# Loading a weight matrix by columns instead of by rows, with a new order of all steps, in a one-core attention and MLP kernel

## The chip, the core and the metric

The kernel runs on one core of one Trainium2 chip. Its time is the device time of one execution in microseconds. The core has five engines that work side by side: PE (TensorE, the matmuls; its weight loads are shown as PEld), DVE (VectorE), ACT (ScalarE), POOL (GpSimd) and SP (SyncE, which here only starts DMA transfers). Each engine goes through its own list of instructions in order. An instruction that needs something from another engine or from a transfer waits on a semaphore, and all that stands behind it on that engine waits with it.

## The reference

Attention in two scales on q, k, v of 8 batches, 8 heads, 576 positions and 64 features, and then an MLP on the 4608 tokens:

```
q_d, k_d, v_d = means of q, k, v over 4 positions        # 144 of 576
out  = repeat(softmax(q_d k_d' / 8) v_d, 4)              # coarse
out += softmax(q k' / 8 where |i - j| < 4) v             # local
x = out as 4608 tokens x 512
h = x @ w_in                                             # 512 x 2048
g = where(h > 0, h, exp(min(h, 0)) - 1)
y = g @ w_out                                            # 2048 x 512
```

All inputs and outputs are float32 in the chip's main memory; the matmuls run on float16.

## The kernel before

**Tiling.** A batch has four pairs of heads (j = 0 to 3), which are transposed, scored and normalised pair by pair. The results go into `xt`, the MLP's input with features on partitions, 512 tokens to a block t; a pair's 128 features are one of four row blocks dc of `w_in`. The first layer of block 0 is made in steps `h.0.i` and the other blocks' in `h.t.i`; the ELU takes `he` and `hg`, and the second layer `y` or, from block 6 on, a form with seven products (`p`, `sm`, `wd`).

**The order.** A string `ORDER` holds 1531 keys, each a step on some engines (`lc.1.0.q`: POOL starts the casting load of batch 1, pair 0, q; `T`: transposes; `fN`, `fna`: normalise batch 0 on DVE and add it into `xt` on POOL; `cv`: POOL's cast of a v). The keys are run from first to last, and this sets the order of the instructions on each engine. A stroke behind a key picks another way to do the step: another engine for an elementwise operation, or transposes by DMA instead of on PE. `SLOTS` tells which buffer each tile takes.

**The first weights.** `WI` holds `w_in` as one float16 tile of 128 partitions x 4 row blocks dc x 2048 columns. The keys `wi.0` to `wi.3` run `load_wi(dc)` (L345): one casting transfer each on POOL's queue, for one row block with all 2048 columns. The order issues them as wi.1, wi.2, wi.0, wi.3. `w_in(dc, fc)` takes 128 columns, four apart, out of the group of 512 columns that `fc // 4` names.

**The partial products ahead.** While batch 0 is still being normalised pair by pair, PE runs the keys `H.0` to `H.3` (`ahead(dc)`, matmuls at L891): for h.0.0 and h.0.1, that is fc 0 to 3, the partial product with row block dc alone. Each is four matmuls of 128 x 256. They read columns 0 to 511 of row block dc. Behind them stand `fO` (the outputs of a pair half), and the transposes `T.1.n` of batch 1.

**Fills.** `Z.0` to `Z.3` (`more_zeros`) are two matmuls of zeros each, 128 x 512, between the first steps on PE; `zeros` begins with thirteen such, and others of the kind (`lg<-Z`) stand in front of some `fO`.

**Semaphores of POOL's loads.** The casting loads that POOL starts take eight semaphores, DMASW0 to DMASW7, in turn. A wait for one of them is a wait for a certain load on it.

Of the kernel before, what the change touches and what calls it, by code (L numbers as in the profile page):

```python
# [41 lines left out]
lc.0.2.q zeros Z.3 lv.0.1 lc.0.2.k empties cIND cN cI cR T.0.2.(0,2) ek.0.2' edges sq.2.q eq.0.2 sk.2.k'  # L42
s.2.1.2 lc.0.1.k lc.0.1.q T.0.1.(0,0) s.2.0.2 lv.0.3 lx.0.0.k lx.0.0.q lx.2.3.q lv.0.0 close eq.0.1' ek.0.1
sk.1.k cx.0.0.k sq.1.q' s.1.0.0 cx.0.0.q T.0.0.(1,0) sq.0.q' ek.0.0' x.2.0 x.1.0 eq.0.0 s.1.1.0 x.1.1 sk.0.k
s.0.0.1 x.0.0 cv.0.3 lc.0.3.q lc.0.3.k wi.1 Z.2 T.0.3.(0,0) sq.3.q' Z.1 eq.0.3' ek.0.3' fD.0.0 Z.0 cVR2 cVR
lv.0.2 cIND2 sk.3.k' s.3.0.1 x.3.0 cv.0.0 cSEL lc.1.0.q wi.2 lc.1.2.q wi.0 wi.3 lc.1.3.q cv.0.1 cv.0.2 fdr.0
# [5 lines left out]
T.1.3 ek.1.3' cv.1.1' eq.1.3 T.1.2 h.0.15 h.0.10 eq.1.2 he.0.8 he.0.15 hg.0.5' sk.1.1 lx.2.0.k sk.1.3 hg.0.15
sq.1.2' lx.2.0.q sq.1.1 sq.1.3 s.1.3 sd.1.3 ek.1.2 he.0.10 x.1.3.0 sk.1.2 hg.0.8 wo.2 sq.1.0 cv.1.2 cv.1.3
lv.2.0 wo.1 cx.2.0.q lx.2.2.q' cx.2.0.k cv.2.0 h.0.3 s.1.1 sd.1.1 x.1.1.0 x.1.1.1 x.1.3.1 h.0.9 he.0.9'
hg.0.10 hg.0.9' s.1.2 sd.1.2 x.1.2.0 m.1.2 m.1.3 m.1.1 fna.2.1' lv.2.2 s.1.0 sd.1.0 h.0.2 x.1.2.1 x.1.0.0
he.0.2 x.1.0.1 he.0.3' m.1.0 hg.0.2 lx.2.2.k hg.0.3' V.1 h.0.11 h.0.12 D.1 vc.1 he.0.11' he.0.12 y.0.0 dr.1
P.1.1 P.1.3 pc.1.3' h.0.4 pc.1.1 P.1.2 on.1.1 of.1.1 hg.0.12 pc.1.2 T.2.0 y.0.1 eq.2.0 ek.2.0 hg.0.11' n.1.1
P.1.0 h.0.14 on.1.3 of.1.3 he.0.4' pc.1.0 he.0.14' y.0.4 y.0.5 on.1.0 of.1.0 a.1.1.1' a.1.1.2' sk.2.0 n.1.3
a.1.3.1' hg.0.4' lv.2.1 lv.3.1 wo.3 cx.2.1.q cx.2.1.k a.1.3.2 fna.3.1 cv.2.1' cx.2.2.q' cx.2.2.k n.1.0 on.1.2
of.1.2 hg.0.14' n.1.2 a.1.2.1' a.1.0.1 lx.2.3.k y.0.6 T.2.1 y.0.7 T.2.2' h.1.0 y.0.2 h.1.1 ek.2.1' yc.0.1'  # L60
eq.2.2 ek.2.2 eq.2.1 he.1.0 s.2.0 lx.3.2.q lx.3.1.k lv.2.3 sq.2.0' sd.2.0 he.1.1' sk.2.2 hg.1.0 sq.2.2'
hg.1.1' sk.2.1 x.2.0.0 s.2.2 y.0.3 h.0.13 lx.3.1.q lx.3.0.k ys.0.1 x.2.0.1 cv.2.2 cx.2.3.q cx.2.3.k cv.2.3'
cx.3.0.k lx.3.0.q lv.3.0 lv.3.2 lx.3.2.k h.1.5 he.1.5 yc.0.0 sq.2.1' hg.1.5 h.1.3 he.1.3' he.0.13 fl.3.0
lx.3.3.k T.2.3 sd.2.2 ek.2.3 a.1.2.2 cx.3.0.q cv.3.0 cx.3.1.k cx.3.1.q a.1.0.2 x.2.2.0 x.2.2.1 y.0.12 hg.0.13
y.0.13 h.1.7 hg.1.3' m.2.0 sk.2.3 m.2.2 he.1.7 cv.3.1' cx.3.2.k cx.3.2.q hg.1.7 y.0.8 s.2.1 sd.2.1 y.0.14
ys.0.0 eq.2.3 x.2.1.0 x.2.1.1 h.1.4 T.3.0 he.1.4' h.1.2 y.0.9 he.1.2' m.2.1 sq.2.3' eq.3.0' hg.1.4' lv.4.0
fl.3.1 lx.3.3.q lv.3.3 lx.4.0.q' lx.4.0.k s.2.3 sd.2.3 T.3.1 sq.3.0 cv.3.2 cx.3.3.k cx.3.3.q fl.3.2 fl.3.3
x.2.3.0 x.2.3.1 hg.1.2' eq.3.1' sq.3.1 m.2.3 h.1.6 y.0.15 T.3.2 D.2 V.2 he.1.6 eq.3.2 hg.1.6 dr.2 h.1.8 vc.2
yc.0.3 P.2.2 P.2.1 h.1.11 pc.2.1' pc.2.2 he.1.8' sk.3.1 hg.1.8' on.2.1 of.2.1 y.1.0 P.2.0 h.1.9 y.0.10
he.1.11' he.1.9' n.2.1 pc.2.0' hg.1.11' on.2.0 of.2.0 s.3.1 sd.3.1 n.2.0 hg.1.9' a.2.0.3' h.1.13 P.2.3 cv.3.3  # L70
a.2.1.3 a.2.0.2 x.3.1.0 x.3.1.1 sk.3.0 lx.4.3.q'' a.2.1.2 pc.2.3 he.1.13' h.1.12 on.2.2 of.2.2 sq.3.2 n.2.2
# [1379 lines left out]
```

## Time and profile before

| What | Value |
|---|---|
| median of 3 runs | 340.17 us (339.78 to 340.57) |
| profiled execution | 339.14 us, span 337.3 us, mean granted PE clock 0.994 |
| PE busy | 326.0 us, 97% of the span |
| DVE busy | 253.1 us, 75% |
| ACT busy | 210.2 us, 62% |
| POOL busy | 165.4 us, 49% |
| moved by DMA | 49.06 MB, 145 GB/s over the span |

The profile comes from one execution. Its own time, 339.14 us, is 1.03 us below the median of the three timed runs, and 1.8 us of it lie outside the span. Busy times of the engines overlap; what counts is which engine has no gap in a stretch, and what ended its gaps where it has some. A row of the windows view gives, for a stretch from A to B, its length and the busy time (with the number of instructions) of PE, PEld, DVE, ACT and POOL, then the granted PE clock, the share of DMA that was busy and the GB/s moved. A row of the timeline gives start, duration, engine, line, operation, out<-in, and in brackets how long the engine stood idle before it and what released it. The profile's line numbers are those of the kernel before; the changed one's are 3 lower there (L888 is L891), and 6 to 8 lower near the end.

### The profile page before, as it was taken

To read this page: it belongs to the slowest core of one execution; us is meant where nothing else is said; L and a number is where in the kernel's file an instruction comes from. 1 tells how busy PE (TensorE), PEld (TensorE's weight loads), DVE (VectorE), ACT (ScalarE), POOL (GpSimd) and SP (SyncE) were. 2 spreads that over 40 slices of the span, in tenths; PEclk is the share of its full clock that TensorE was granted. 3 is DMA by queue.
4 is the path that set the end of the run, shared out by engine and by line. 5 is a ranking of instruction groups with operands and counts; after the bars stand their busy time and mean duration, and the time that the engine had idled before them with its cause. 6 is when DMAs were issued, how large, how long until landed. Compare 5 with 4: busy or idle time off the path is not lost.

```text
span 337.3 us, 10747 instructions
## 1 busy us (share of the span) xinstructions
PE 326.0 (97%) x4418; PEld 194.3 (58%) x4418; DVE 253.1 (75%) x495; ACT 210.2 (62%) x369; POOL 165.4 (49%) x261
## 2 busy tenths in 40 slices
...
GB/s 166 232 207 205 193 202 207 199 220 168 188 190 203 136 235 187 157 216 195 165 175 201 175 201 173 109 168 76 31 67 92 65 31 2 0 127 0 1 126 124
DMA packets 109746, 49.06 MB, mean 145 GB/s; under 512 B 93937, under 2 KB 104193, under 8 KB 109697
## 3 DMA queue, kind: packets, MB, share of 16 engines
...
q0 software_dynamic: 5312, 7.15, 12.8%
q8 instruction: 34, 0.56, 0.7%
q10 hardware_dynamic: 240, 0.11, 0.2%
q14 instruction: 15, 0.12, 0.1%
...
## 4 chain that ended last, share of the span: by engine, by line
PE 72%; DVE 8%; DMA 7%; POOL 5%; issue 4%; SPq 2%; ACT 1%; DVEq 0%; POOLq 0%; ACTq 0%
PE hp L915 30%; PE op L956 20%; PE y L1028 6%; PE xz L1028 5%; DMA q<-in_q_dram 5%; DMA v<-in_v_dram 2%; PE lg L795 2%; DVE gt L946 2%; PE den L703 1%; PE sc L643 1%; SPq L452 1%; DVE xt L879 1%; POOL v L477 1%; PE hp L891 1%; DVE e L945 1%
## 5 line engine op out<-in xcount | busy, mean ns | idle before, releaser
L915 PE MATMUL hp<-xt,WI 128*128 128x512 f16 x512 | 127.7, 381 | 0.4 <-DVE gt L946 0.3
L956 PE MATMUL op<-WO,gt 128*128 128x512 f16 x384 | 95.1, 379 | 0.4 <-DVE gt L946 0.4
L915 PEld LDWEIGHTS <-WI 128*128 128x128 f16 x512 | 55.3, 114 | 44.4 <-issue 1.1
L941 DVE SCALAR_TENSOR_TENSOR gt<-e,hp 128x512 f16<-128x512 f16 x76 | 51.6, 682 | 23.6 <-ACT e L937 23.5
L936 ACT ACTIVATE r<-hp 128x512 f32<-128x512 f32 x76 | 45.4, 597 | 35.3 <-PE hp L915 34.1
L926 ACT ACTIVATE e<-hp 128x512 f16<-128x512 f32 x68 | 40.3, 597 | 32.0 <-PE hp L915 30.4
L956 PEld LDWEIGHTS <-gt 128*128 128x128 f16 x384 | 36.0, 98 | 41.6 <-DVE gt L946 1.1
L937 ACT ACTIVATE e<-r 128x512 f16<-128x512 f32 x76 | 47.9, 631 | 2.4
L946 DVE SCALAR_TENSOR_TENSOR gt<-hp,e 128x512 f16<-128x512 f32 x68 | 47.0, 692 | 2.7
L879 POOL TENSOR_TENSOR xt<-ln 128x128 f16<-128x128 f16 (+7 forms) x35 | 24.0, 695 | 42.6 <-DVE ln L868 42.6
L945 DVE TENSOR_SCALAR e<-e 128x512 f16<-128x512 f16 x68 | 24.2, 356 | 20.9 <-ACT e L926 20.6
L666 ACT ACTIVATE pex<-sc 128x580 f16<-128x580 f32 (+1 forms) x56 | 31.2, 596 | 6.8 <-PE sc L656 6.7
L1006 POOL TENSOR_TENSOR s<-gt 128x512 f16<-128x512 f16 x8 | 9.4, 1176 | 34.4 <-DVE gt L941 12.3
L415 POOL CAST k<-k 96x768 f16<-96x768 f32 x22 | 18.3, 831 | 15.8 <-DMA k<-in_k_dram 15.8
L477 POOL CAST v<-v 128x640 f16<-128x640 f32 (+1 forms) x19 | 14.1, 744 | 23.2 <-DMA v<-in_v_dram 23.0
L415 POOL CAST q<-q 96x768 f16<-96x768 f32 x20 | 16.6, 832 | 12.6 <-DMA q<-in_q_dram 8.7
L1028 PEld LDWEIGHTS <-gt 128*128 128x128 f16 x192 | 18.8, 98 | 4.8
L868 DVE TENSOR_TENSOR ln<-lg,rcb 128x580 f16<-128x580 f32 x28 | 21.0, 751 | 0.0
L561 DVE TENSOR_REDUCE ke<-kt 128x145 f16<-128x580 f16 x28 | 20.8, 750 | 0.0
L891 PE MATMUL hp<-xt,WI 128*128 128x256 f16 x128 | 16.3, 274 | 1.5 <-DVE gt L946 0.9
L579 POOL TENSOR_TENSOR t<-qt 128x288 f32<-128x288 f16 x16 | 10.6, 665 | 13.0 <-DVE qt L543 8.1
L1028 PEld LDWEIGHTS <-s 128*128 128x128 f16 x144 | 14.1, 98 | 3.4
...
## 6 DMA issues: line engine op xcount, KB each, us to landing
v<-in_v_dram SPq DMA_DIRECT2D x111, 80.0 KB, 4.8
...
WI<-in_moe_w_in_dram POOLq DMA_DIRECT2D x4, 512.0 KB, 8.9
WO<-in_moe_w_out_dram POOLq DMA_DIRECT2D x4, 512.0 KB, 6.4
```

Source lines behind the costliest of these rows:

```text
L415: nc.gpsimd.tensor_copy(out=x[:], in_=src)
L666: nc.scalar.activation(out=s["p"][:, :, a : a + n], in_=g2(sc, a, n), func=AF.Exp, scale=SCALE / 16 if a else SCALE,)
L879: (eng or nc.gpsimd).tensor_tensor(out=xt(t)[:, j, t0 - TBLK * t : t1 - TBLK * t], in0=ln[:, a:z], in1=_rep4(ln[:, ga : ga + (z - a) // 4] ...
L915: nc.tensor.matmul(hp, w_in(dc, fc), xts[t][:, dc, :], start=(dc == 0), stop=(dc == DMC - 1),)
L926: nc.scalar.activation(out=e, in_=hp, func=AF.Exp)
L936: nc.scalar.activation(out=r, in_=hp, func=AF.Relu, scale=-1.0)
L937: nc.scalar.activation(out=e, in_=r, func=AF.Exp, scale=-1.0)
L941: nc.vector.scalar_tensor_tensor(out=to, in0=e, scalar=-1.0, op0=AB.add, in1=hp, op1=AB.max)
L945: nc.vector.tensor_scalar(out=e, in0=e, scalar1=1.0, scalar2=-1.0, op0=AB.min, op1=AB.add)
L946: nc.vector.scalar_tensor_tensor(out=to, in0=hp, scalar=0.0, op0=AB.max, in1=e, op1=AB.add)
L956: nc.tensor.matmul(op_[:], gts[t][:, fc, 128 * tt : 128 * tt + 128], WO[:, fc, :], start=(fc == 0), stop=(fc == FCN - 1),)
L1028: nc.tensor.matmul(to, w, x, start=(k == 0 and n in (1, 2)), stop=(k == FH - 1), skip_group_check=n > 2,)
```

## The change

`load_wi(n)` now loads a group of 512 columns over all four row blocks, in place of a row block over all columns. The fills `Z` are gone. The order of all steps is another one, 278 steps have another form, and the buffers follow. Four keys go (the fills), so 1527 are left. The order now issues wi.0 first, then wi.2 and wi.3, and wi.1 last.

```
     def load_wi(dc):
-        nc.gpsimd.dma_start(out=WI[:, dc, :], in_=moe_w_in[128 * dc : 128 * dc + 128])
+        n = slice(512 * dc, 512 * dc + 512)
+        nc.gpsimd.dma_start(out=WI[:, :, n], in_=moe_w_in[:, n].rearrange("(c p) f -> p c f", p=128))
...
-    def more_zeros(n):
-        keep(two("zf"), 2)
-
...
-    for n in range(4):
-        at("Z", more_zeros, n)
...
 ORDER = """
-fD.2.0 fN.1 fdr.2 H.0 H.1 fna.1.0 lc.1.1.k fD.3.0 fP.2.0 fO.2.0 fpc.2 fdr.3 fN.2 fna.2.0 lc.1.2.k H.2 H.3
-fP.3.0 h.0.0 h.0.7 fO.3.2 h.0.1 he.0.0 fpc.3' hg.0.0 fN.3 he.0.7 he.0.1' T.1.0 h.0.5 cv.1.0 fna.3.0 wo.0
+s.3.1.0 fD.1.0 fD.2.0 fN.0 fna.0.0 x.3.1 lv.1.3 fdr.1 fdr.2 fP.1.1 fD.3.0 fV.2 H.0 fP.2.0 fpc.2 lx.2.1.q fdr.3
+fvc.2' fpc.1' fO.1.4 fN.1 fO.3.2 fP.3.0 fpc.3 fN.3 fna.1.0 cv.1.0 wi.1 H.1 H.2 H.3 fO.2.0 T.1.1 h.0.0 h.0.1
```

**On PE, at the partial products.** WI is the weight, xt the moving operand, hp the partial product; DMASW names the semaphore of the load that is waited for. Before, H.0 waits for wi.0 (DMASW2), H.1 for wi.1 (DMASW6), H.2 for wi.2 (DMASW0) and H.3 for wi.3 (DMASW3):

```order
L748 MATMUL den<-pex,IND 32x72
L891 LDWEIGHTS WI [waits DMASW2_49]
L891 MATMUL hp<-xt,WI 128x256 [waits Pool_49]
...
L891 LDWEIGHTS WI [waits DMASW6_49]
...
L834 MATMUL lg<-pex,vd 64x72
L891 LDWEIGHTS WI [waits DMASW0_49]
L891 MATMUL hp<-xt,WI 128x256 [waits Pool_49]
...
L891 LDWEIGHTS WI [waits DMASW3_49]
```

Now H.0 waits for wi.0 alone (DMASW6), and the first weights of H.1 wait for three semaphores:

```order
L888 LDWEIGHTS WI [waits DMASW6_49]
L888 MATMUL hp<-xt,WI 128x256 [waits Pool_49]
...
L760 MATMUL rb<-rch,SEL 128x72
L888 LDWEIGHTS WI [waits DMASW7_49,DMASW6_49,DMASW1_49]
L888 MATMUL hp<-xt,WI 128x256
...
L824 MATMUL lg<-pex,v_459 64x96 [waits DVE_49]
...
L505 LDWEIGHTS q_475 [waits DMASW2_49]
```

What moved: H.0 stands by itself earlier, and H.1, H.2 and H.3 stand together behind fP.3.0 (the rb matmuls), ahead of fO.2.0 (lg) and the first transposes of batch 1 (tqk). The wait of H.1 names the semaphores that wi.3 (DMASW7), wi.2 (DMASW6) and wi.1 (DMASW1) use; no first-layer weight behind it waits for a load of WI.

**On POOL, at the loads of WI.** xt<-ln is fna, CAST v is cv, the 1x1 COPY belongs to cv. Before, all four pieces are issued ahead of the first fna; the three that follow wi.1 stand like this:

```order
L374 DMA q_534<-in_q_dram 96x2x384 [waits DMASW0_49,PE_49]
L345 DMA WI<-in_moe_w_in_dram 128x2048
L374 DMA q_537<-in_q_dram 96x2x384 [waits DMASW3_49,DMASW1_49,PE_49]
L345 DMA WI<-in_moe_w_in_dram 128x2048 [waits DMASW2_49]
L345 DMA WI<-in_moe_w_in_dram 128x2048
L374 DMA q_541<-in_q_dram 96x2x384 [waits DVE_49,DMASW4_49,PE_49,Activation_49]
```

Now wi.2, wi.3 and wi.1 stand like this:

```order
L342 DMA WI<-in_moe_w_in_dram 128x4x512 [waits DMASW6_49]
L342 DMA WI<-in_moe_w_in_dram 128x4x512 [waits DMASW7_49]
L371 DMA q_490<-in_q_dram 96x2x384 [waits DMASW0_49]
L851 ISA
L851 TENSOR_TENSOR xt<-ln 128x2x288 [waits DVE_49] x2
L474 CAST v_847<-v_503 128x640 [waits DMAHW6_49,DMAHW7_49,DMAHW1_49,DMAHW0_49]
L401 COPY apart<-v_847 1x1 [waits Pool_49]
L342 DMA WI<-in_moe_w_in_dram 128x4x512 [waits DMASW1_49]
```

What moved: the last piece, wi.1, went behind both fna.0.0 and fna.1.0, which wait for DVE's fN.0 and fN.1, and behind the cast cv.1.0.

More of the change, by code (lines that the diff above doesn't have):

```diff
@@ L41 @@
 ORDER = """
[L42 to L46, printed above, removed]
@@ L52 @@
[L52 to L56, printed above, removed]
@@ L57 @@
[L57 to L71, printed above, removed]
@@ L147 @@
-sm.8.2.3' pk.8.0.7' sm.8.3.3' pf.8.1.4 pk.8.0.1 p.8.0.6.0 p.8.0.4.0 p.8.1.5.0 p.8.0.6.1 pk.8.0.6' p.8.1.5.1
-pf.8.1.5 p.8.0.4.1 p.8.0.5.0 p.8.0.5.1 ps.8.1.5 pf.8.0.4 pf.8.0.5 ps.8.0.5 p.8.1.3.0 p.8.1.3.1 pf.8.1.3
-ps.8.1.3 p.8.0.3.0 p.8.0.3.1 pf.8.0.3 ps.8.0.3
+lc.0.2.q cI lc.0.2.k cR zeros T.0.2.(0,2) lx.0.0.q eq.0.2 empties ek.0.2' edges sq.2.q cN cVR2 lx.0.0.k cVR
+cIND2 lv.0.0 sk.2.k' lc.0.1.q lc.0.1.k s.2.0.2 T.0.1.(0,0) lc.0.3.k lc.0.3.q s.2.1.2 close eq.0.1' sk.1.k'
+cx.0.0.k ek.0.1' sq.1.q x.2.0 cx.0.0.q T.0.0.(1,0) sq.0.q' eq.0.0' s.1.0.0 ek.0.0 x.1.0 s.1.1.0 sk.0.k
@@ new lines @@
+he.0.1 he.0.0' lv.1.2 fN.2 ek.1.1' fna.3.0' eq.1.1' sq.1.1 lx.2.3.q' fna.2.0 fna.2.1 T.1.0 h.0.5 he.0.5'
+hg.0.1 hg.0.0' lx.2.0.q cMASK lx.3.1.q sk.1.1 fna.3.1' ek.1.0 sk.1.0 hg.0.5' h.0.7 T.1.3 eq.1.3 eq.1.0 h.0.6
+T.1.2 ek.1.2' wo.1 wo.0 sq.1.3 cv.1.1 ek.1.3 he.0.6' h.0.8 h.0.15 he.0.8 eq.1.2 he.0.15 sq.1.2 sq.1.0 lv.2.0
+sk.1.3 hg.0.6' lx.2.0.k s.1.1 sd.1.1 s.1.3 cv.1.2 cv.1.3 hg.0.8 lx.2.2.k hg.0.15 sk.1.2 lv.2.1 lx.2.1.k cFOUR
+cx.2.0.q sd.1.3 h.0.10 h.0.12 x.1.3.0 x.1.1.0 x.1.3.1 x.1.1.1 he.0.7 wo.2 cx.2.0.k cv.2.0 hg.0.7 s.1.0 s.1.2
@@ new lines @@
+sd.1.0 he.0.12 he.0.10 x.1.0.0 hg.0.10 lx.2.2.q' h.0.9 he.0.9' h.0.3 sd.1.2 hg.0.9' x.1.0.1 x.1.2.0 he.0.3'
+m.1.0 m.1.3 m.1.1 hg.0.3' hg.0.12 V.1 h.0.2 h.0.11 y.0.0 x.1.2.1 m.1.2 D.1 he.0.11' hg.0.11' dr.1 he.0.2'
+vc.1' hg.0.2' h.0.4 P.1.3 P.1.1 pc.1.3' h.0.14 he.0.4' pc.1.1 on.1.1 of.1.1 n.1.1 y.0.1 P.1.0 pc.1.0 T.2.0
+on.1.3 of.1.3 hg.0.4' a.1.1.1' n.1.3 ek.2.0 eq.2.0 sq.2.0' sk.2.0 a.1.1.2' a.1.3.2' y.0.4 P.1.2 wo.3 cx.2.1.q
+cx.2.1.k cv.2.1' cx.2.2.q' cx.2.2.k a.1.3.1 pc.1.2 he.0.14' lv.3.1 lx.2.3.k lv.2.2 lx.3.1.k on.1.2 y.0.5
@@ new lines @@
+on.2.0 of.2.0 h.1.9 he.1.9 yc.0.3 s.3.1 sd.3.1 h.1.13 y.1.0 n.2.0 hg.1.9 sk.3.2 a.2.0.3' a.2.1.3 a.2.0.2
+a.2.1.2 lx.4.2.k' fl.3.3 lv.4.1 lx.4.1.k' lx.4.1.q on.2.2 of.2.2 x.3.1.0 he.1.13' x.3.1.1 n.2.2 h.1.12 he.1.12
+hg.1.13' hg.1.12 P.2.3 pc.2.3 y.0.11 s.3.0 sd.3.0 on.2.3 of.2.3 m.3.1 n.2.3 x.3.0.0 x.3.0.1 cv.3.3 cx.4.0.k
+cx.4.0.q a.2.2.2 h.1.14 he.1.14 y.1.1 T.3.3 h.1.10 eq.3.3 hg.1.14 sk.3.3 he.1.10' hg.1.10' sq.3.3 a.2.3.3
+s.3.2 h.1.15 s.3.3 sd.3.3 sd.3.2 a.2.3.2 he.1.15' x.3.3.0 x.3.2.0 y.1.2 h.2.0 hg.1.15' m.3.0 x.3.2.1 x.3.3.1
@@ new lines @@
+h.2.8 he.2.8' cv.4.0' yc.0.2' y.1.3 T.4.0' ys.0.3 eq.4.0'' lx.4.2.q fl.4.0 lv.4.2 m.3.3 m.3.2 yc.1.0' cx.4.1.k
+cx.4.1.q cv.4.1 cx.4.2.k cx.4.2.q T.4.1'' V.3 vc.3' he.2.0' hg.2.0' hg.2.8' D.3 sq.4.0' dr.3 fl.4.1' y.1.4
+y.1.5 h.2.4 y.1.6 eq.4.1 s.4.1 h.2.5 he.2.4' sq.4.1 lx.4.3.k lx.5.3.q' y.1.7 sk.4.1 hg.2.4' he.2.5 h.2.1
+cv.4.2' yc.1.1 he.2.1 cx.4.3.k hg.2.5 sk.4.0 y.1.8 so.3 ys.0.2 lv.4.3 si.3 s.4.0 sd.4.1 sd.4.0 h.2.2 y.1.12
+cx.4.3.q' x.4.1.0 hg.2.1 he.2.2 x.4.1.1 hg.2.2 x.4.0.0 cv.4.3' x.4.0.1 h.2.7 T.4.2'' h.2.10 m.4.0 on.3.0
@@ new lines @@
+he.3.1 hg.3.1 cx.5.3.k a.3.3.4 cx.5.3.q a.3.1.4 h.3.15 y.2.10 he.3.15 so.4 T.5.3' ys.1.2 eq.5.3'' lx.6.0.q'
+si.4 fl.5.3 lv.6.1 ys.2.1 on.4.0 of.4.0 of.4.3 y.2.13 h.3.7 he.3.7' hg.3.15 n.4.3 sq.5.3' hg.3.7' h.3.5
+he.3.5' s.5.0 sd.5.0 n.4.0 hg.3.5' y.2.11 h.3.11 y.2.14 h.3.8 on.4.2 he.3.11 x.5.0.0 x.5.0.1 on.4.1 of.4.1
+of.4.2 yc.2.2' he.3.8' hg.3.11 a.4.0.5' a.4.3.5 sq.5.2 cv.5.3' cx.6.0.k' cx.6.0.q sq.5.1 lx.7.0.q'' a.4.0.4
+hg.3.8' n.4.2 h.3.10 he.3.10' hg.3.10' a.4.3.4' sk.5.3 m.5.0 y.2.15 y.3.4 yc.2.3 h.3.12 y.3.0 he.3.12' s.5.1
@@ new lines @@
+ys.2.3 fl.6.2 ys.3.0 fl.6.1 hg.4.2 dr.5 sq.6.0 h.4.1 vc.5 he.4.1 yc.3.1 hg.4.1 h.4.4 y.3.12 y.3.8 h.4.10
+y.3.13 he.4.4' he.4.10 hg.4.4' hg.4.10 h.4.11 he.4.11 hg.4.11 s.6.0 sd.6.0 x.6.0.0 h.4.3 x.6.0.1 he.4.3' y.3.9
+h.4.7 T.6.3 so.5 lx.7.3.q' sk.6.1 hg.4.3' on.5.0 of.5.0 h.4.5 y.3.10 y.3.11 lv.7.0 si.5 eq.6.2'' ys.3.1 fl.6.3
+he.4.7 he.4.5 eq.6.3' m.6.0 sk.6.2 hg.4.7 h.4.9 he.4.9 hg.4.5 yc.3.2' h.4.8 y.3.14 y.4.0 he.4.8' cv.6.3'
+cx.7.0.k fl.7.0 lv.7.1 cx.7.0.q' T.7.0'''' eq.7.0 hg.4.9 n.5.0 hg.4.8' h.4.14 a.5.0.6 a.5.0.5' on.5.3 on.5.1
@@ new lines @@
+of.5.1 of.5.3 he.4.14' n.5.1 n.5.3 h.4.12 he.4.12' hg.4.12' hg.4.14' a.5.3.5 sq.6.2' sk.6.3 a.5.1.5 a.5.1.6
+sq.7.0' sq.6.3 y.3.15 y.4.1 s.6.1 sd.6.1 yc.3.3 on.5.2 of.5.2 h.4.15 y.4.2 n.5.2 cv.7.0' he.4.15' x.6.1.0
+x.6.1.1 hg.4.15' a.5.2.5' y.4.4 h.4.13 he.4.13 y.4.5 s.6.3 s.6.2 sd.6.2 sd.6.3 hg.4.13 lx.7.3.k lx.7.1.q'
+h.5.0 h.5.2 y.4.3 y.4.6 x.6.3.0 he.5.0 he.5.2 m.6.3 x.6.2.0 x.6.2.1 x.6.3.1 yc.4.0 hg.5.0 m.6.2 m.6.1 hg.5.2
+sk.7.0 h.5.1 y.4.7 he.5.1 V.6 D.6 dr.6 hg.5.1 h.5.7 lv.7.2 lx.7.2.k lx.7.1.k ys.3.2 lv.7.3 cx.7.1.k cx.7.1.q
@@ new lines @@
+on.6.2 on.6.3 of.6.2 of.6.3 h.5.15 yc.4.2 yc.4.3 he.5.15' h.5.11 he.5.11' sk.7.3 a.6.1.6' n.6.3 a.6.0.6
+hg.5.15' n.6.2 hg.5.11' sk.7.1 y.5.0 y.5.1 h.5.12 he.5.12' y.5.2 h.5.14 ys.4.2 hg.5.12' wd.2.2' wd.0.0'
+he.5.14 hg.5.14 sk.7.2 sq.7.1 sq.7.3 wd.0.3 a.6.3.7 a.6.3.6 sq.7.2 a.6.2.6 s.7.1 sd.7.1 s.7.3 sd.7.3 x.7.1.0
+x.7.1.1 x.7.3.0 y.5.4 h.6.0 he.6.0' s.7.2 sd.7.2 h.6.1 a.6.2.7' hg.6.0' y.5.5 h.6.3 x.7.3.1 he.6.1 he.6.3
+x.7.2.0 hg.6.1 hg.6.3 m.7.2 m.7.1 m.7.3 y.5.6 y.5.7 h.6.4 yc.5.1 x.7.2.1 he.6.4 closeturn h.6.2 D.7 V.7 hg.6.4
@@ new lines @@
+hg.7.2 sm.7.0.0 pk.6.1.6 h.7.15 h.7.8 he.7.8 p.6.0.7.0 h.7.13 p.6.0.5.0 p.6.0.7.1 p.6.0.5.1 he.7.15' hg.7.8
+pk.6.0.7' hg.7.15' pf.6.0.5 p.6.1.7.1 he.7.13 pk.6.1.7 h.7.9 he.7.9' sm.6.1.3' sm.6.0.3 sm.6.2.3 a.7.3.8
+p.6.1.4.0 hg.7.13 p.6.1.5.0 p.6.1.5.1 h.7.7 pf.6.1.5 p.6.1.4.1 p.6.0.4.0 he.7.7 h.7.10 p.6.0.4.1 h.8.0
+he.7.10' pf.6.1.4 hg.7.7 hg.7.9' hg.7.10' p.6.0.3.0 p.6.0.3.1 h.7.11 he.8.0 sm.7.3.0 sm.7.1.0 sm.7.1.2
+sm.7.1.3 hg.8.0 he.7.11 hg.7.11 sm.7.1.1 p.6.1.3.0 h.8.2 p.6.1.3.1 sm.7.0.1' pf.6.0.3 pf.6.1.3' h.8.4 he.8.4
```

176 lines of the change are left out of this document (76 added, 100 removed).

## The prediction

> **What bounds the kernel now.** I read the page's busy times first, then the windows view in twelve stretches, then the timelines of PE and POOL in the first 42 us, and last the groups by line and form for prices.
>
> ```profile
> span 337.3 us, 10747 instructions
> PE 326.0 (97%) x4418; PEld 194.3 (58%) x4418; DVE 253.1 (75%) x495; ACT 210.2 (62%) x369; POOL 165.4 (49%) x261
> PE 72%; DVE 8%; DMA 7%; POOL 5%; issue 4%; SPq 2%; ACT 1%; DVEq 0%; POOLq 0%; ACTq 0%
> ```
>
> PE is busy nearly throughout and holds 72% of the chain that ends last. The windows say where that is true:
>
> ```profile
> 9.00:12.40 3.40, 1.69 (x34) 1.10 (x34) 0.98 (x10) 0.32 (x1) 2.12 (x4) 1.00 1.14 258
> 12.40:15.90 3.50, 3.50 (x50) 2.42 (x44) 1.50 (x4) 1.63 (x4) 0.50 (x2) 0.51 1.34 208
> 24.00:32.70 8.70, 7.99 (x177) 5.18 (x176) 5.16 (x14) 4.08 (x6) 3.44 (x5) 1.00 1.17 210
> 32.70:38.00 5.30, 5.24 (x110) 4.44 (x111) 3.97 (x7) 2.07 (x4) 3.98 (x7) 1.00 1.25 181
> 38.00:60.00 22.00, 19.58 (x464) 16.40 (x459) 19.75 (x40) 19.46 (x36) 12.25 (x24) 1.00 1.08 208
> 60.00:110.00 50.00, 49.14 (x830) 27.05 (x832) 43.68 (x74) 38.97 (x69) 34.30 (x64) 1.00 1.07 194
> 110.00:230.00 120.00, 119.99 (x1622) 61.50 (x1611) 95.55 (x178) 76.51 (x133) 50.61 (x96) 1.00 0.98 178
> 230.00:333.00 103.00, 103.00 (x956) 66.80 (x955) 78.17 (x152) 60.62 (x110) 47.98 (x48) 1.00 0.16 50
> ```
>
> From 110 to 333 us PE has no gap at a full clock (1.00): there only matmul work counts, and a step moved between ACT, DVE and POOL is hidden by PE as long as PE is fed. Idle time of PE that an order can win or lose lies ahead of 110 us: 0.86 us in 60 to 110, 2.42 in 38 to 60, and little in 32.7 to 38. In 12.4 to 15.9 us the clock was 0.51, behind a stretch in which PE was busy for half the time. So the forecast rests on the first 60 us, and on whether PE's total work changes.
>
> **The change part by part.** *1. The wait of H.1.* The program's order shows that H.1's first weights now wait for wi.3, wi.2 and wi.1, though they lie in columns 0 to 511, which wi.0 brings. A piece by columns covers all four row blocks, so the span of addresses of wi.1 to wi.3 crosses row block 1, and the wait is set by it. H.1 can therefore not start before the last piece has landed, and that piece now stands on POOL behind fna.0.0, fna.1.0 and cv.1.0. Behind H.1 on PE stand H.2, H.3, fO.2.0, T.1.1 and everything after: scores, h.0 steps, transposes; ACT and DVE wait for those. When does wi.1 land? These are the rows of the corresponding steps before: DVE's fN.1, POOL's two fna, cast, copy, and the landing times of the loads.
>
> ```profile
> 32.17 0.91 DVE L846 TENSOR_TENSOR ln<-lg,rcb 128x720 f16<-128x720 f32 x1 [0.81 <-PE lg L834]
> 31.52 1.19 POOL L854 TENSOR_TENSOR xt<-ln 128x576 f16<-128x576 f16 x1
> 33.33 1.19 POOL L854 TENSOR_TENSOR xt<-ln 128x576 f16<-128x576 f16 x1
> 37.98 0.73 POOL L477 CAST v<-v 128x640 f16<-128x640 f32 x1
> 38.77 0.18 POOL L404 COPY apart<-v 1x1 f16<-1x1 f16 x1
> L345 POOL DMA_DIRECT2D WI<-in_moe_w_in_dram x4: 556/577/585, 12.3 to 20.4; - x4
> ...
> DMA to landing us min/median/max: 6.3/8.9/10.4
> WO<-in_moe_w_out_dram POOLq DMA_DIRECT2D x4, 512.0 KB, 6.4
> ```
>
> (The sixth and seventh row are of the four loads of WI.) fN.1 ended at 32.17 + 0.91 = 33.08 us. In the new order the front gets there sooner; what can be won shows in these rows:
>
> ```profile
> 11.96 0.45 PE L508 MATMUL tq<-ID,q 96*64 96x96 f16 x12 [1.63 <-DMA q<-in_q_dram]
> 10.28 0.83 POOL L477 CAST v<-v 112x768 f16<-112x768 f32 x1 [6.29 <-DMA v<-in_v_dram]
> 11.05 0.63 POOL L374 DMA_DIRECT2D q<-in_q_dram  x1
> L1073 PE MATMUL zf<-Z 128*128 128x512 f16 x8 | 2.4, 383 | 0.0
> ```
>
> PE stood 1.63 us for the second q. Now this q is POOL's third load, not its fourth, and the cast of v, for which POOL stood 6.29 us with lc.0.3 behind it, comes after lc.0.3. At a half clock 3.50 us of work would take 1.75 less. The eight fills that go are 8 x 383 ns = 3.06 us of PE, at most 2.3 of them (six) ahead of the first normalise. Together 1.63 + 1.75 + 2.3 = 5.7; not all of it lies on the path, and I put the upper bound at 5. Below: POOL now issues 17 loads ahead of fna.0.0 in place of 15, 2 x 0.63 = 1.3 us, so the lower bound is -1.3. I take 2.0, nearest to the wait of 1.63 that surely has a cause less. fN.1 then ends at 31.1. On POOL follow a hand-over of 0.1, fna.1.0 with 1.2, the cast with 0.8 (37.98 to 38.77) and the copy with 0.2: wi.1 is issued at 33.4. For its landing there are 6.3 to 10.4 us. I take the 6.4 of WO, which was likewise issued with few loads of POOL ahead of it (the four of WI were issued from 12.3 to 20.4, with q loads between): 39.8 us. What that costs is read off the first transposes of batch 1:
>
> ```profile
> 34.98 1.06 PE L891 MATMUL hp<-xt,WI 128*128 128x256 f16 x8
> 35.88 0.49 PE L763 MATMUL rb<-rch,SEL 112*128 112x72 f16 x10
> 36.20 1.04 PE L891 MATMUL hp<-xt,WI 128*128 128x256 f16 x8
> 37.08 0.59 PE L1073 MATMUL lg<-Z 128*128 128x512 f16 x2
> 37.61 0.32 PE L827 MATMUL lg<-pex,v 112*64 112x96 f16 x6
> 38.02 0.42 PE L508 MATMUL tqk<-ID,q 96*64 96x96 f16 x12
> 38.28 0.42 PE L508 MATMUL tqk<-ID,k 96*64 96x96 f16 x12
> ```
>
> Eight matmuls of H took 35.88 - 34.98 = 0.90 us from start to start, so the twelve of H.1 to H.3 take 1.35; one fO took 38.02 - 37.61 = 0.41. T.1.1 then starts at 39.8 + 1.35 + 0.41 = 41.56. Before, batch 1's first transposes started at 38.02, with h.0.7 done (37.08 - 36.20 = 0.88), which now comes later: 37.14 for the same work. **The hold costs 41.56 - 37.14 = +4.4 us.** By its bounds: each us that the front wins takes one off (+1.4 at 5, +7.7 at -1.3), and a landing of 8.9 or 10.4 in place of 6.4 adds 2.5 or 4.0.
>
> *2. The clock behind the hold.* PE is done with everything ahead of H.1 at about 32 us (the rb matmuls of fP.3.0 need only what fN.1 needed and one more reciprocal), so it stands some 8 us. The windows show 0.51 for 3.5 us behind a lighter gap than that: 1.71 us of 3.40. Bounds: nothing, if PE waits for other engines then anyway (2.42 idle in 38 to 60), to 3.50 x (1 - 0.51) = 1.7 us. I take +1.2, nearer to the upper, since PE was 89% busy in 38 to 60 (19.58 of 22).
>
> The Trainium skill (TensorE: Matmul & The Clock Gate, Part 1, "The HAM clock gate (the "warmup" mystery)") says that a window of about 3.4 us without work halves PE's clock, and that it takes about as long of steady work to get it back. The trace agrees on the 0.51 and on its length of 3.5 us. By that rule alone a hold of 8 us costs up to 1.7 us, against the 1.2 of my sum; and the rule speaks against taking out the fills, which are there between PE's first steps.
>
> *3. More transposes on PE.* Two loads of batches 1 to 7 that went through DMA transposes go over PE now: 12 more of the 64-row form and 6 of the 128-row form.
>
> ```profile
> L508 PE MATMUL tqk<-ID,q 96*64 96x96 f16 x96 | 3.5, 209 | 0.0
> L513 PE MATMUL tqk<-ID,k 96*128 96x96 f16 x30 | 2.1, 206 | 0.0
> ```
>
> By busy time 12 x 3.5/96 + 6 x 2.1/30 = 0.86 us at most, where PE has no gap; two blocks of twelve lay 38.28 - 38.02 = 0.26 apart in the timeline, so I take +0.6 (bounds 0.3 and 0.86).
>
> *4. The shape of the pieces.* A piece now is 512 rows of 512 values in place of 128 rows of 2048. No row of before shows a casting load with so short rows; the bounds are those of the landing times, in item 1.
>
> *5. Elementwise work in other places.* Twelve ELU steps go from one form to the other, some copies from ACT to DVE, ten or so steps to POOL. They lie under PE from 110 us on (95.55 of 120 is DVE's share there, the highest). If that cover were gone, a DVE step more would cost its 692 ns. In the tail, one copy `ou<-y` is on the other engine (418 against 369 ns).
>
> ```profile
> L946 DVE SCALAR_TENSOR_TENSOR gt<-hp,e 128x512 f16<-128x512 f32 x68 | 47.0, 692 | 2.7
> L1051 ACT COPY ou<-y 128x256 f32<-128x256 f32 x4 | 1.5, 369 | 6.5 <-PE y L1028 6.5
> L1051 DVE COPY ou<-y 128x256 f32<-128x256 f32 x2 | 0.8, 418 | 0.3 <-PE y L1028 0.3
> ```
>
> I take 0 for all of it, with bounds of -1 and +1.
>
> The sum on the profiled execution: 339.14 + 4.4 + 1.2 + 0.6 = 345.3 us. The median of the runs is 1.03 above that execution, so the forecast is **346.4 us**, +1.8%.
>
> **The rivals.**
>
> *Paid back between 38 and 110 us (the other side).* While PE stands, the loads go on (about 200 GB/s in every row up to 110) and ACT and DVE empty their queues, so PE's later gaps, 2.42 + 0.86 = 3.28 us, vanish, and with them the felt part of the slow clock. With the front at its bound of 5: 339.14 + 1.4 - 3.28 + 0.6 = 337.9, or **338.9** by the median. It decides once the front wins more than 4.4 us; below that the kernel is the same or slower. For it: the DMA engines are never idle there. Against it: in 38 to 60 DVE and ACT are 90% and 88% busy, and their work comes from PE, which is what stands.
>
> *A shorter hold.* The front wins 4 to 5 us and nothing is paid back, or wi.1 lands in less than 6 us: +1.4 to +2.4 for the hold, 0.6 to 1.2 for the clock, 0.6: 341.8 to 343.3, or about **343** by the median.
>
> *wi.1 stands behind other loads.* wi.2, wi.3 and lc.1.2.q are issued close ahead of it on the same queue, as three of the four WI loads were before. With 8.9 to 10.4 us from issue to landing the hold grows by 2.5 to 4.0: **348.9 to 350.4**.
>
> *The slow clock lasts longer.* In the slow stretch the chain's rows show mostly transposes, and the clock stayed down through all of them:
>
> ```profile
> 12.41 0.32 PE tk L508 x12
> 12.73 0.72 PE tq L530 x12
> 13.45 0.72 PE tk L530 x12
> 14.17 0.97 PE sc L1073 x2
> ```
>
> Behind the hold T.1.1, T.1.0 and T.1.3 follow. If the clock stays down for twice the 3.5 us, another 1.7 us is lost: **348.1**. The Trainium skill (the same page, Part 4, "PE-mode transpose") has the rule that a transpose doesn't count as work for the clock in the way of a matmul.
>
> *The pieces do not matter to H.1.* This would need wi.1 to be there when PE comes to H.1 at 32, so issued by 25.6; POOL's fna.1.0 waits for fN.1, so I give it no chance of its own.
>
> **How the numbers follow.** The likeliest case, a hold of 3 to 6 us (own range 343.5 to 348.7), has 0.56. A shorter hold 0.13, longer by the queue 0.13, by the clock 0.05. Paid back in full and faster 0.08; a front and a payback that just cancel the hold, within 0.2%, 0.05. A difference of 0.2% (0.7 us) is about what a measurement of this kernel can tell from none. So faster 0.08, same 0.05, slower 0.87. The range 341 to 350.5 leaves out the two cases of the other side and the upper end of the queue's, and holds 0.82 or so.
>
> **What would show it.** Right: a gap of PE at L888 of 5 to 10 us, released by the DMA of WI, somewhere between 30 and 42 us, with H.1 starting at 39 to 41; POOL's last WI issue behind two fna and a cast at about 33; the granted clock at half for about 3.5 us behind the gap; T.1.1 at 40 to 43; fN.1 ending near 31; no gap of PE beyond 110 us. Wrong: a gap of PE at H.1 below 2 us, an issue of wi.1 ahead of 28 us, or gaps of PE in 38 to 110 that are smaller than before by as much as the hold is long. If the time is slower and the loss lies behind 110 us, items 3 and 5 are wrong and not item 1.

## The result, and the profile after

The changed kernel takes 351.84 us (median of 4 runs, 350.92 to 353.05), against 340.37 for the kernel before: a ratio of 1.0312 (95% interval 1.0223 to 1.0402). That is slower, as forecast, but by 11.5 us and not by 6.2, and above the range. Executions of the kernel before spread from 338 to 349 us; the ratios leave out those more than 1.5% above the fastest, but the slowest of the four here, 344.49 us, is just inside, and without it the ratio would be 1.0345.

The profiled execution took 353.05 us (span 350.9, mean granted clock 0.983), 13.9 us more than the one before; it is the slowest of its four, 1.2 us above their median. The windows view of the changed kernel, same columns as before:

```profile
32.70:38.00 5.30, 1.07 (x31) 0.84 (x30) 1.45 (x3) 0.76 (x1) 2.81 (x4) 1.00 1.02 190
38.00:42.00 4.00, 0.00 (x0) 0.00 (x0) 0.00 (x0) 0.00 (x0) 0.00 (x0) 0.57 1.11 198
42.00:50.00 8.00, 6.17 (x88) 4.98 (x89) 2.51 (x4) 1.71 (x3) 0.00 (x0) 0.58 0.04 8
50.00:60.00 10.00, 9.30 (x207) 7.99 (x205) 9.76 (x22) 9.51 (x19) 9.05 (x16) 1.00 0.74 158
...
110.00:243.00 133.00, 132.07 (x1824) 68.29 (x1824) 105.86 (x190) 83.32 (x147) 61.71 (x112) 1.00 0.90 174
```

From 38 to 42 us PE, DVE, ACT and POOL all stand. From 42 to 50 the loads stand too (8 GB/s): SP started none between 39.4 and 51.9 us, since its next load of q waited 12.4 us for DVE, which stood as well. The clock is at 0.57 and 0.58. In that stretch lie the rows that the forecast named; first PE's timeline:

```profile
33.29 0.48 PE L760 MATMUL rb<-rch,SEL 112*128 112x72 f16 x10
43.78 2.75 PE L888 MATMUL hp<-xt,WI 128*128 128x256 f16 x12 [10.01 <-DMA WI<-in_moe_w_in_dram]
46.47 0.45 PE L824 MATMUL lg<-pex,v 112*64 112x96 f16 x6
...
47.20 0.68 PE L505 MATMUL tqk<-ID,q 96*64 96x96 f16 x12
...
48.40 0.61 PE L505 MATMUL tqk<-ID,q 96*64 96x96 f16 x12
48.82 0.45 PE L505 MATMUL tqk<-ID,k 96*64 96x96 f16 x12
49.20 1.06 PE L888 MATMUL hp<-xt,WI 128*128 128x256 f16 x8
```

PE waits 10.01 us at H.1 for a load of WI. Then H.1 to H.3 take 46.47 - 43.78 = 2.69 us, fO.2.0 takes 0.73, and T.1.1 starts at 47.20. POOL's timeline shows why wi.1 came so late:

```profile
27.11 1.17 POOL L851 TENSOR_TENSOR xt<-ln 128x576 f16<-128x576 f16 x1 [2.09 <-DVE v L446]
33.32 1.17 POOL L851 TENSOR_TENSOR xt<-ln 128x576 f16<-128x576 f16 x1 [5.04 <-DVE ln L843]
34.43 0.72 POOL L474 CAST v<-v 128x640 f16<-128x640 f32 x1
35.21 0.18 POOL L401 COPY apart<-v 1x1 f16<-1x1 f16 x1
35.45 0.79 POOL L342 DMA_DIRECT2D WI<-in_moe_w_in_dram  x1
```

POOL stood 5.04 us for fN.1, and issued wi.1 at 35.45. The chain of waits has the landing:

```profile
35.45 8.29 DMA WI<-in_moe_w_in_dram
43.74 0.04 issue
```

The last block on PE ended at 345.12 + 1.91 = 347.03 us, against 331.62 + 1.91 = 333.53 before; what follows it in the span is nearly equally long (3.9 and 3.8 us). So 13.5 us of the 13.9 arose while PE ran. Of them 10.06 (47.20 against the 37.14 worked out for the same work) stood before batch 1's transposes began, and 3.4 arose behind that point. These are the timelines' last rows, the changed kernel's first, then the one before:

```profile
345.12 1.91 PE L1025 MATMUL y<-WO,s 128*128 128x256 f16 x16
```

```profile
331.62 1.91 PE L1028 MATMUL y<-WO,s 128*128 128x256 f16 x16
```

### The profile page after: what moved, and what is told of

Same layout as the page of the kernel before. It is cut to its first block, busy times and chain, and to the rows that moved or that the text cites. A ratio compares the mean times of both kernels' runs of the same rounds, so it can differ in the third digit from the quotient of the medians.

```text
span 350.9 us, 10765 instructions
## 1 busy us (share of the span) xinstructions
PE 326.4 (93%) x4428; PEld 194.7 (55%) x4428; DVE 256.8 (73%) x494; ACT 203.8 (58%) x361; POOL 176.2 (50%) x275
## 4 chain that ended last, share of the span: by engine, by line
PE 74%; DMA 8%; DVE 5%; ACT 5%; issue 3%; POOL 2%; SPq 1%; POOLq 0%; ACTq 0%
PE hp L912 31%; PE op L953 21%; PE y L1025 5%; DMA v<-in_v_dram 5%; PE xz L1025 4%; PE hp L888 3%; DMA WI<-in_moe_w_in_dram 2%; PE lg L792 2%; PE sc L640 2%; DVE e L942 1%; PE lg L812 1%; PE tqk L510 1%; PE tqk L505 1%; DMA q<-in_q_dram 1%; ACT r L933 1%
## 5 line engine op out<-in xcount | busy, mean ns | idle before, releaser
L912 PEld LDWEIGHTS <-WI 128*128 128x128 f16 x512 | 55.3, 114 | 45.9 <-issue 2.5
L923 ACT ACTIVATE e<-hp 128x512 f16<-128x512 f32 x80 | 47.3, 599 | 55.9 <-PE hp L912 42.7
L876 POOL TENSOR_TENSOR xt<-ln 128x384 f16<-128x384 f16 (+7 forms) x42 | 29.5, 716 | 69.5 <-DVE ln L865 69.3
L943 DVE SCALAR_TENSOR_TENSOR gt<-hp,e 128x512 f16<-128x512 f32 x80 | 55.3, 692 | 3.1
L938 DVE SCALAR_TENSOR_TENSOR gt<-e,hp 128x512 f16<-128x512 f16 x64 | 43.4, 681 | 17.2 <-ACT e L934 16.9
L933 ACT ACTIVATE r<-hp 128x512 f32<-128x512 f32 x64 | 38.3, 599 | 28.8 <-PE hp L912 24.9
L942 DVE TENSOR_SCALAR e<-e 128x512 f16<-128x512 f16 x80 | 34.3, 429 | 22.0 <-ACT e L923 21.8
L934 ACT ACTIVATE e<-r 128x512 f16<-128x512 f32 x64 | 40.4, 631 | 2.0
L576 POOL TENSOR_TENSOR t<-qt 128x288 f32<-128x288 f16 x19 | 12.7, 667 | 21.6 <-DVE qt L540 14.2
L888 PEld LDWEIGHTS <-WI 128*128 128x128 f16 x128 | 13.9, 118 | 13.1 <-DMA WI<-in_moe_w_in_dram 10.1
L961 ACT COPY os<-op 128x512 f32<-128x512 f32 x19 | 11.0, 587 | 9.2 <-PE op L953 9.2
```

The costliest lines, as they stand in the source:

```text
L876: (eng or nc.gpsimd).tensor_tensor(out=xt(t)[:, j, t0 - TBLK * t : t1 - TBLK * t], in0=ln[:, a:z], in1=_rep4(ln[:, ga : ga + (z - a) // 4] ...
L888: nc.tensor.matmul(FS[i][:, 256 * f : 256 * f + 256], w_in(dc, 2 * n + f), xts[0][:, dc, 256 * h : 256 * h + 256], start=(f == dc == 0), s ...
L912: nc.tensor.matmul(hp, w_in(dc, fc), xts[t][:, dc, :], start=(dc == 0), stop=(dc == DMC - 1),)
L923: nc.scalar.activation(out=e, in_=hp, func=AF.Exp)
L933: nc.scalar.activation(out=r, in_=hp, func=AF.Relu, scale=-1.0)
L934: nc.scalar.activation(out=e, in_=r, func=AF.Exp, scale=-1.0)
```

## The experiments

**Theory.** The hold at H.1 costs the time: its wait for all pieces, with the last one issued late, and the half clock behind it. **Rivals.** The new order is slow elsewhere; the shape of the pieces is slow by itself; the idle time is paid back later.

**1. Four tiles.** The changed kernel, its order as it is, with a tile for each group of columns. H.1 then waits for nothing but the piece that it reads.

```
-    WI = sb.tile([128, DMC, DFF], FP16, tag="WI", ...)
+    WI = [sb.tile([128, DMC, 512], FP16, tag=f"WI{i}", ...) for i in range(4)]
-        a = 512 * (fc // 4) + fc % 4
-        return WI[:, dc, a : a + 509 : 4]
+        a = fc % 4
+        return WI[fc // 4][:, dc, a : a + 509 : 4]
-        nc.gpsimd.dma_start(out=WI[:, :, n], ...)
+        nc.gpsimd.dma_start(out=WI[dc][:], ...)
```

> The changed kernel with its order as it is, but WI as four tiles of 512 columns, so that H.1 waits for nothing but what it reads (wi.0); wi.1, issued as late as before, is waited for only by h.0.3 and its like, later on PE. If the wait across pieces is the cause: no gap of PE at H.1 beyond 1 us, T.1.1 at about 36, no stretch of half clock behind it, and 351.8 - 11.3 = about 340.5 us, as fast as the kernel before. If the late load as such (its traffic, or the loads behind it) costs the time: 346 us or more. If the new order is itself better than the old by what the front wins, below 339.7.

Measured: 342.59 us, ratio to before 1.0065 (1.0016 to 1.0113). PE's timeline of this run:

```profile
32.88 0.60 PE L888 MATMUL hp<-xt,WI 128*128 128x256 f16 x4
33.82 1.03 PE L888 MATMUL hp<-xt,WI 128*128 128x256 f16 x8 [0.34 <-POOL xt L851]
...
35.30 0.45 PE L505 MATMUL tqk<-ID,q 96*64 96x96 f16 x12
...
333.57 1.91 PE L1025 MATMUL y<-WO,s 128*128 128x256 f16 x16
```

The gap is gone, though wi.1 is issued about as late as in the changed kernel. T.1.1 starts 47.20 - 35.30 = 11.90 us earlier, and PE ends 347.03 - 335.48 = 11.55 earlier. So the hold, with its clock, is worth 9.25 us by the medians, 8.4 by the two ratios to the kernel before (2.47%; the changed kernel was timed on another occasion than the experiments) and 11.55 by the profiles (of the slowest of four executions and the second fastest of ten), and nearly nothing of it is paid back later. The time is 2 us above what was expected. What is left over the kernel before is 0.65%, or 335.48 - 333.53 = 1.95 us of PE's time. It does not arise at the front: T.1.1 starts 37.14 - 35.30 = 1.84 us earlier than the kernel before would reach it with the same work done. So by these two traces the new order gains 1.84 us up to T.1.1 and loses 3.8 us behind it, with no hold and a mean clock of 0.999. The numbers of matmuls on PE bear out that the work is the same: 3878 from T.1.1 to the end, against 3852 from 38.02 on, 8 of h.0.7 and the 18 transposes that were added.

**2. Rows again.** The changed kernel with the load by rows put back and nothing else.

```
-        n = slice(512 * dc, 512 * dc + 512)
-        nc.gpsimd.dma_start(out=WI[:, :, n], ...)
+        nc.gpsimd.dma_start(out=WI[:, dc, :], in_=moe_w_in[128 * dc : 128 * dc + 128])
```

> The changed kernel with the load by rows put back and nothing else. H.1 then reads row block 1, which only wi.1 brings, and wi.1 is issued as late as before: the wait is a true one now. If the late issue in the new order is what costs, whatever the shape of the pieces: the same gap of 8 to 10 us at H.1 and 351 to 352 us. If the column shape of the pieces carries a part of the loss: 350 us or less, by as much as this part.

Measured: 352.48 us, ratio 1.0299 (1.0212 to 1.0387), with this row in PE's timeline:

```profile
42.30 2.75 PE L887 MATMUL hp<-xt,WI 128*128 128x256 f16 x12 [9.32 <-DMA WI<-in_moe_w_in_dram]
```

The same hold, now for data that H.1 really needs. The clock came back sooner, at 46.15 us (a block of transposes takes 0.42 us from there on), 3.85 us behind the gap. So the shape of the pieces costs nothing that can be seen: the order that issues the last piece behind both fna needs H.1 to be free of that piece, and neither form of the load in one tile frees it.

**3. The last piece early.** In the order, `wi.1` goes from behind `cv.1.0` to behind `wi.3`.

```
-fna.1.0 cv.1.0 wi.1 H.1 H.2 H.3
+fna.1.0 cv.1.0 H.1 H.2 H.3
-wi.2 wi.3 lc.1.2.q
+wi.2 wi.3 wi.1 lc.1.2.q
```

> The changed kernel with one key moved: wi.1 is issued right behind wi.3, ahead of lc.1.2.q and of both fna; the wait of H.1 for three pieces stays. In the changed kernel wi.3 landed at 33.7 us and the q behind it at 36.2, so wi.1 should land at about 36, PE's gap at H.1 should shrink from 10.0 to 2 to 3 us, and T.1.1 start at about 38 in place of 47.2. If the place of wi.1 behind POOL's fna is the cause: 351.8 - 9.4 = about 342.4 us. If the new order loses its time elsewhere, or the loss is in the shape of the pieces: 348 us or more.

Measured: 348.15 us, ratio 1.0227 (1.0150 to 1.0305). PE's timeline:

```profile
37.52 2.75 PE L888 MATMUL hp<-xt,WI 128*128 128x256 f16 x12 [4.61 <-DMA WI<-in_moe_w_in_dram]
...
40.93 0.68 PE L505 MATMUL tqk<-ID,q 96*64 96x96 f16 x12
...
43.23 3.41 PE L888 MATMUL hp<-xt,WI 128*128 128x256 f16 x16
46.58 0.45 PE L505 MATMUL tqk<-ID,q 96*64 96x96 f16 x12
...
340.74 1.91 PE L1025 MATMUL y<-WO,s 128*128 128x256 f16 x16
```

The gap shrank to 4.61 us, not to 2 or 3, and the time by 3.7 us (2.9 by the ratios), not by 9.4. Against the run with four tiles T.1.1 is 5.63 later and PE's end 342.65 - 335.48 = 7.17. The difference of 1.54 is the clock: sixteen matmuls of a step that took 1.94 us there (37.94, below) took 3.41 here, and PE was back at full clock only at 46.6, 9.1 us behind the gap. So in this execution half the gap cost no less in clock than the whole one. It is not so in each: the mean clocks of the four timed runs go from 0.985, which is this one, to 0.995. By an estimate from these (twice the missing share of the span) the half clock lasted from some 10 us down to 3.4. The gap stayed above what was expected because wi.1, issued at 23.6 right behind wi.2 and wi.3, landed at 37.5 and not at 36, 13.9 us behind its issue. This is the row of the run with four tiles:

```profile
37.94 1.94 PE L888 MATMUL hp<-xt,WI 128*128 128x256 f16 x16
```

**4. The hold filled.** Matmuls of zeros between fP.3.0 and H.1, first forty, then twenty-eight.

```
-cv.1.0 wi.1 H.1
+cv.1.0 wi.1 ZF.0 ZF.1 H.1
+    def hold_fill(n):
+        keep(two("zf"), 20)      # 14 in the second
```

> The changed kernel with forty matmuls of zeros (128 x 512) on PE between fP.3.0 and H.1: the hold stays as long, but PE is busy in it. If the slow clock behind the hold is a part of the cost: the granted clock stays near 1.0 from 38 to 50 us, H.1 to H.3 take 1.35 in place of 2.69 us and fO.2.0 0.41 in place of 0.73, T.1.1 starts at 45.5, and the time falls by 2 to 2.5 us to about 349.5. If the clock costs nothing that other waits would not have cost: within 0.7 us of 351.8.

> As the run with forty matmuls of zeros in the hold, with twenty-eight: forty took from 35.2 to 45.5 us and so ended 3 us behind wi.1's landing at 42.6, which hid what a full clock would give. Twenty-eight end at about 42.5. If the slow clock behind the hold costs time: H.1 starts at 43, T.1.1 at about 44.7 in place of 47.2, and the kernel takes about 349.3 us, 2.5 less than the changed one. If it costs nothing in the end: 351.8 within 0.7.

Measured: 352.02 us with forty, ratio 1.0350 (1.0289 to 1.0410), and 349.25 with twenty-eight, 1.0203 (1.0130 to 1.0276). The fills of the first ran until 45.55 and held H.1 themselves, 1.77 us longer than the load does in the changed kernel. PE's timeline of the first, then that of the second and a window of it:

```profile
45.55 1.47 PE L888 MATMUL hp<-xt,WI 128*128 128x256 f16 x12
...
49.17 1.94 PE L888 MATMUL hp<-xt,WI 128*128 128x256 f16 x16
```

```profile
34.70 6.20 PE L1070 MATMUL zf<-Z 128*128 128x512 f16 x28 [1.86 <-DVE v L446]
42.34 1.50 PE L888 MATMUL hp<-xt,WI 128*128 128x256 f16 x12 [1.43 <-DMA WI<-in_moe_w_in_dram]
...
45.98 1.94 PE L888 MATMUL hp<-xt,WI 128*128 128x256 f16 x16
```

```profile
42.00:50.00 8.00, 6.72 (x128) 5.95 (x129) 5.58 (x10) 4.60 (x9) 2.57 (x4) 1.00 0.07 10
```

The clock stays at 1.00, H.1 to H.3 take 1.50 and not 2.75 us, and the time falls by 2.6 us by the medians, as expected (3.7 by the ratios). Not all of this is the clock: in the profiled execution H.1 also started 43.78 - 42.34 = 1.44 us earlier, since wi.1 was there earlier. The clock's share is read from H.1's start to the next step of sixteen matmuls: 49.20 - 43.78 = 5.42 us at half clock, 45.98 - 42.34 = 3.64 and 49.17 - 45.55 = 3.62 at the full one. That is 1.8 us. The run with forty agrees: it starts H.1 1.77 us later, wins 1.80 by the clock, and takes as long as the changed kernel (352.02 against 351.84).

**5. Columns in the kernel before**, in one tile and then in four; the order of before.

```
-        nc.gpsimd.dma_start(out=WI[:, dc, :], ...)
+        n = slice(512 * dc, 512 * dc + 512)
+        nc.gpsimd.dma_start(out=WI[:, :, n], ...)      # second run: out=WI[dc][:], with four tiles
```

> The kernel before with the load by columns alone, its order as it was. H.1 then waits for all four pieces too, but these are issued by 20.4 us and landed by 30, ahead of H.0 at 32.8. If only the wait together with the late issue costs time: the same as before, within 0.7 us. If pieces of shorter rows cost by themselves (four times as many rows for the same bytes): landing times above 10.4 us, a gap at H.1, and 1 us or more on top.

> The kernel before with the load by columns into four tiles: H.0 to H.3 wait for wi.0 alone. Beside the run with columns in one tile (+1.0%, with a wait of 2.1 us for a k at 43 us and a slow clock behind it) this tells the shape of the pieces from the wait across them. If the wait across pieces cost that 1%: the same as before, within 0.7 us. If pieces by columns keep POOL's queue of loads longer, so that the k loads behind them land later: again 342.5 to 344 us, with k landing at 44 in place of 42.7.

Measured: 343.59 us in one tile, ratio 1.0104 (1.0051 to 1.0157); 343.28 in four, 1.0002 (0.9942 to 1.0062). Neither has a gap at H.1 beyond 0.3 us. The loads of WI landed in 7.4 to 11.9 us in the first and 6.8 to 10.6 in the second, against 6.3 to 10.4 before. The first had this row, and a slower clock behind it (0.83 from 42 to 50 us):

```profile
45.87 0.45 PE L509 MATMUL tqk<-ID,k 96*64 96x96 f16 x12 [2.11 <-DMA k<-in_k_dram]
```

Pieces by columns cost nothing measurable in four tiles. The one tile was expected to take as long as the kernel before and took 1% longer. Whether that is its own or the luck of that k load is not settled: its four runs (342.8 to 344.1) lie at and just above the upper end of what the four tiles' runs in the ratio spread over (338.9 to 343.6).

**6. The fills `Z` taken out of the kernel before.**

```
     def more_zeros(n):
-        keep(two("zf"), 2)
+        turns.append(turns.pop(0))      # only the buffers' turn
```

> The kernel before without the eight matmuls of zeros of Z.0 to Z.3; the buffers turn as if they were there, and nothing else changes. If these fills only fill PE's waits and the clock does not need them: the same as before within 0.7 us. If they hold the clock up, as a rule on idle windows would have it: the half clock of 12.4 to 15.9 us gets longer or a second such stretch comes, +1 to +2 us. If they stand in the way of the front: up to 2 us faster.

Measured: 343.11 us (11 runs, 338.07 to 348.03), ratio 0.9975 (0.9912 to 1.0039). No difference that can be measured, so these eight fills neither hold the clock up nor stand in the way. The trace kept of this run has a clock of 0.50 from 12.4 to 24 us, but so has that of the four tiles of experiment 5, which keep the fills.

**7. What is left over.** Four tiles again, and beside it four tiles with three steps back in their old form.

```
-T.4.2'' fl.4.2'' eq.4.2   T.6.3  eq.6.3'   sm.8.3.1
+T.4.2   fl.4.2   eq.4.2'  T.6.3' eq.6.3''  sm.8.3.1'
```

> The changed kernel with WI in four tiles once more, to be compared with the one beside it and with the kernel before on one chip. By its first run: 342.6 us, 0.65% (0.16 to 1.13) above the kernel before. If the new order is worth something once the hold is gone: at or below the kernel before.

> The changed kernel with WI in four tiles (which took the hold away and left 0.65% over the kernel before), and three steps back in their old form: the transposes of T.4.2 and T.6.3 by DMA again (12 of the 18 added to PE), and the step sm.8.3.1 on DVE instead of POOL, for which PE stood 0.5 us near the end. If what is left over comes from such steps: 12/18 of 0.86 us and 0.5 us less, 1.1 us below the same kernel without them in the same call, and no wait of PE for POOL's gt. If it comes from the order in many small places: no difference beyond 0.5 us, with other small waits in place of these.

Measured: four tiles 343.06 us, ratio 1.0053 (1.0015 to 1.0091); with the steps back 342.69, 1.0019 (0.9981 to 1.0057). PE's two longest waits beyond 110 us, four tiles first:

```profile
PE hp L912 <- DVE gt L943: 1.0, 1, 1.0
PE xz L1025 <- POOL gt L1003: 0.5, 1, 0.5
```

```profile
PE hp L912 <- DVE gt L943: 1.7, 5, 0.7
PE sc L640 <- DVE ln L865: 1.0, 1, 1.0
```

The four tiles are slower than before by half a per cent a second time. The three steps seem to take 0.34% off, the 1.1 us expected, but the intervals overlap, and the wait for POOL's gt made room for others. In the trace of the four tiles PE also had a stretch of half clock without a hold, behind waits of 0.5 and 1.1 us, of which the longer is put down to no engine and no load. It costs 1.5 us there (sixteen matmuls took 3.47 us in place of 1.94):

```profile
32.70:42.00 9.30, 7.37 (x121) 5.58 (x118) 7.15 (x13) 4.23 (x7) 6.13 (x11) 0.82 1.19 210
```

What the new order loses behind T.1.1 against the one trace of the kernel before is 6.4 us here, the clock's 1.5 among it, 5.2 with the three steps back, and 3.8 in experiment 1. The 3.8 are 1.5 us more busy time of PE, the added transposes' 0.86 among it, and 2.3 us more of small gaps; which steps cause them stays open. No version here is measurably faster than the kernel before.

## Why the prediction was right in direction and wrong in size

**The wait at H.1 (item 1): right.** H.1 waited for the last piece, issued behind both fna and the cast, and PE with all behind it stood. The run with four tiles takes just that wait away and with it 9.25 of the 11.5 us by the medians.

**The size of the hold: too small, by 5.6 us up to T.1.1.** It started at 47.20, not at 41.56, so the +4.4 should have been 10.06. Three terms of the sum were mis-sized, by about as much each:

- *The issue of wi.1*, 33.4 forecast, 35.45 measured (2.05). The step that failed here is "I take 2.0" for the front. These are DVE's two normalisations, fN.0 and fN.1, in the changed kernel:

```profile
26.11 0.91 DVE L843 TENSOR_TENSOR ln<-lg,rcb 128x720 f16<-128x720 f32 x1 [0.76 <-PE lg L831]
...
32.33 0.91 DVE L843 TENSOR_TENSOR ln<-lg,rcb 128x720 f16<-128x720 f32 x1 [1.93 <-PE lg L831]
```

  and fN.0 in the kernel before:

```profile
29.64 0.91 DVE L846 TENSOR_TENSOR ln<-lg,rcb 128x720 f16<-128x720 f32 x1 [0.53 <-PE lg L834]
```

  fN.0 ended 30.55 - 27.02 = 3.5 us earlier, so the front did gain, and the half clock of 12.4 to 15.9 us is gone (1.00 there now). But fN.1 ended at 33.24, against 33.08: the new order puts the last scores of pair 3, the fD of three pairs, fP.2.0 and H.0 between the two. I priced the gain of the front as one number, and it did not reach the step that releases wi.1. The size varies: in the traces of the experiments with the new order fna.1.0 started at 32.3 to 33.2 us and not at 33.32, so that up to 1.1 of the 2.05 belongs to this execution.
- *Its landing*, 6.4 taken, 8.29 measured (1.9). I chose WO's row over WI's own 8.9; the rival of a slower landing had this right. What made it slow stays open; right behind wi.2 and wi.3, in experiment 3, it took 13.9.
- *H.1 to H.3 and fO.2.0 at half clock*, 1.35 and 0.41 taken, 2.69 and 0.73 measured (1.7). I had the slow clock begin behind the hold's first work, as an item of its own; it began inside the hold, between 38 and 42 us.

**The clock (item 2): right in kind, somewhat too small.** 1.2 us forecast, 1.8 by the rows of experiment 4, of which the 1.7 above are a part. The Trainium skill (TensorE: Matmul & The Clock Gate, Part 1, "The HAM clock gate (the "warmup" mystery)") says that a window of about 3.4 us without work halves PE's clock, and that it takes about as long of steady work to come back. The hold agrees with the first: PE stood from 33.77 us, and the clock was 1.00 until 38 and 0.57 from 38 to 42. But experiment 7 has a half clock behind waits of 0.5 and 1.1 us only. The second agrees in experiment 2, with 3.85 us. It does not here, with 48.8 - 43.8 = 5.0, nor in experiment 3, with 9.1; transposes and short matmuls are among the work in all three. My reading of the rule, that it speaks against taking out the fills, was not borne out for `Z` (experiment 6).

**Transposes and moved steps (items 3 and 5): too small.** 0.6 and 0 forecast. With four tiles, where no hold covers it, the order loses 3.8 us or more behind T.1.1 (experiments 1 and 7). In the changed kernel 13.5 - 10.06 = 3.4 us arose there, where I had 1.2 and 0.6. So the sum for the profiled execution comes out: 6.2 forecast, 5.6 more up to T.1.1, 1.6 more behind it, and 13.5 measured on PE. The cover of PE that I named from 110 us on has small gaps now: 132.07 busy of 133 in 110 to 243, against none before.

**The shape of the pieces (item 4): right as far as it is shown.** There is nothing to see in experiment 2 and in the four tiles of experiment 5; the 1% of the one tile there stays open.

**The rivals.** Paid back: no; PE's end moved by 11.55 of the 11.90 that T.1.1 moved. A hold whose cause was the queue and a longer clock, each given a small chance, both came true in part, and together; I had treated them as apart and cut the range at the first. With the front's 2.05 us gained the time would have been about 349.8, still above the own range of 343.5 to 348.7.
